# Store order, weight preparation and early splits around the attention bursts and the last quads of a fused attention and two-layer feed-forward kernel

## The chip, the cores and the metric

One core of a Trainium2 chip runs the whole program. TensorE (PE) multiplies, VectorE (DVE) and ScalarE (ACT) do the element-wise work, and one DMA queue, issued by SyncE (SP), moves everything between DRAM and on-chip memory. The metric is the device time of one execution in microseconds. Three runs of the kernel before gave a median of 1045.58 us (1045.37 to 1046.80).

## The reference

Attention over chunks of 32 queries with 16 keys to the left, 8 to the right and 8 memory keys, then two feed-forward layers over 3072 tokens:

```python
scores = scale * q_c @ k_full.T; a = exp(scores - max); a = a / (sum(a) + 1e-09)
x = (a @ v_full) as 3072 x 512
h = x @ w_in;  x = (s * max(h, 0)**2 + b) @ w_out          # 512 -> 2048 -> 512
h = x @ w_in2; out = (h - tanh(h)) @ w_out2                # 512 -> 2048 -> 512
```

## The kernel before, in words

Every float32 product is made of three TensorE products of rounded parts (`three`, lines 238 to 241): high weight by high input, low weight by high input, high weight by low input. So each operand is first split into a rounded high part on ACT and the remainder on DVE. The first two of the three need only the high part of the input, the third its low part. Large products use a seven-product scheme (P1 to P7) instead of eight; the combinations of weights and inputs that it needs are made on DVE.

Four stages follow one another. First attention runs in 24 units of 128 queries, side by side with **up 1** (x by w_in, ReLU, square). Then **down 1** multiplies the squares by w_out, **up 2** by w_in2 with tanh, and **down 2** by w_out2. Every engine works its own instructions in the order in which the program lists them; this order is written out by hand, there is no scheduler. A wait on one engine therefore holds all that stands behind it on that engine.

**START** (lines 38 to 54) is a list of tokens, one step each, for units 0 to 17 and the first 36 turns of up 1. `F` is the product of one turn (12 matmuls), `r` its ReLU on ACT, `Q` its square (on ACT for the turns of SCALAR_SQUARES, else on DVE), `k` and `K` the two halves of a combination on DVE, `st` the store of four squared turns. `wl`, `ws`, `wf`, `wd`, `wc` and `ww` prepare w_in2: load of a raw block, scaling on ACT, filling on DVE, a store, four sums on DVE in the raw block's place, and a store of these. `wr` is `w1_sums` (line 973): five DVE instructions that combine one block of w_in into tile Z8, and a store of it.

**The loop** at line 1066 makes the turns n = 36 to 79 of up 1. At the turns of BURSTS (44, 51, 58, 65, 70) `burst` (line 514) puts a block of attention in front of the turn: scores of two units on PE, their masks on DVE (line 395), the value products of two earlier units on PE, then the transposes of two units on PE. Transposes go into the PSUM banks of the new scores, so they wait until the masks have read these. P2_STEPS gives the turns at which the remaining w_in2 blocks are loaded, scaled, filled and summed; QUADRANTS the turns at which a block of w_out is loaded (with its place), begun on ACT and ended on DVE. EXTRAS holds single steps, among them `w1_sums` 6 and 7 at turns 38 and 41, and `ws_high`, `ws_low` of the first quad at turn 78.

**The quads** (line 1173) make the last part of up 1 by the seven-product scheme, s = 0 to 3. The squares of quad s are written into tiles `oa` and `ob`; there are two pairs of these tiles, so quad 3 writes where quad 1 wrote and must wait until the stores of quad 1 have landed. The stores of quad s - 1 are issued by `combos(1)` inside quad s, four DMAs of 384 and 512 KB. `copy(3)` writes into `oa` and reads a PSUM bank that the product P3 then adds to, so P3 waits for it. `load_to` loads parts of down 1 (1 MB each in two DMAs, `load1`, line 882) into four places, B_STREAM.

**Down 1** takes each part in two halves ("entries"). `split` rounds a half on ACT (line 762) and makes the remainder on DVE (line 763) into a ring of three places, B_RING; `multiply` is 12 matmuls per entry. Entries 0 and 1 use the first half of the weights, entries 2 and 3 the second, made by `high` on ACT and `low` on DVE. `run` (line 811) splits entries 0 to 2, multiplies entry 0, then calls `between1`, which finishes quad 3 with six DVE instructions, and then splits entry 3.

Of the kernel before, what the change touches and what calls it, by code (L numbers as in the profile page):

```python
# [8 lines left out]
F32 = mybir.dt.float32  # L9
# [36 lines left out]
st0 vv8 E11 M12 V7 S13 o7 T9 Q8 M13 r11 R13 F12 F13 E13 l7 qk15 X7 R10 Q11 qk14 K1 C9 wl1 F14 S15  # L46
vv11 D13 D11 L7 M15 R15 S14 Q9 Q10 ws1 r13 r12 M14 V9 E15 V8 T13 T11 st1 wf1 F15 C11 wc1 qk17 r14
D15 k2 Q12 V11 Q14 S17 r15 X11 L11 wl0 vv13 F18 M17 ww1 wd1 F17 R17 E10 Q13 D10 K2 Q15 X9 C13 X8 r17
T10 L9 T15 C10 R14 vv10 V13 L8 V10 k3 C15 r18 K3 F16 r16 R12 F21 wl2 X10 st2 E12 F19 Q16 L10 Q18 Q17
wr4 r19 r21 F20 F24 Q19 wr5 r20 E14 F22 r22 qk16 D12 st3 Q20 F23 r23 Q21 ws2 F25 k4 Q22 F26 ws0 Q23  # L50
wf2 K4 r24 r26 F27 wd2 st4 D14 k5 r25 K5 Q24 wc2 F28 Q25 Q26 r27 F29 ww2 st5 Q27 F30 r29 r28 Q29 k6
K6 r30 st6 Q28 F31 F32 X13 Q30 r31 L13 T12 T14 Q31 r32 k7 K7 Q32 F35 r35 F34 Q35 C12 r34 F33 vv12
Q34 wf0 r33 st7 wc0 S16 V12 Q33 k8 K8 wd0 ww0 st8 X12 M16 L12 R16 C14
"""

WEIGHTS2 = {
# [47 lines left out]
PLAIN_EXPONENTIALS = set()  # L104

P2_STEPS = {}
for m, at in ((3, (42, 45, 46, 50)), (4, (50, 53, 54, 57)), (5, (57, 60, 61, 64)), (6, (64, 67, 68, 71)),
              (7, (71, 74, 75, 78))):
    for step, n in zip(("load", "scaled", "filled", "sums"), at):
        P2_STEPS.setdefault(n, []).append((step, m))  # L110

# [1 line left out]
PLACE_IN_ORDER = list(range(UP_FIRST, 72)) + list(range(80, 88))  # L113
BURSTS = {44: 18, 51: 20, 58: 22, 65: 24, 70: 26}
QUADRANTS = {
    37: ("E8", 40, 41), 45: ("E9", 48, 49), 53: ("E8", 55, 56), 59: ("E9", 61, 62), 66: ("E8", 68, 69),
    73: ("E9", 76, 77), 78: ("E9", None, None),
}
QUADRANT_BEGINS = {x[1] for x in QUADRANTS.values()}
# [33 lines left out]
def tile_chunk_attention_two_ffn(  # L153
# [42 lines left out]
    def new(place, n, dt, name):  # L196
        assert n <= SIZE[place[0]], (place, n)
        if place[0] in "QSRYWV":
            assert place[0] in side["letters"], place
        pool = arena if place[0] in "EZ" else side["of"]  # L200
        return pool.tile([P, n], dt, tag=place, name=name)
# [41 lines left out]
    def scaled(z, raw):  # L243

        hi32 = raw.rearrange("p (n two) -> p n two", two=2)[:, :, 1]
        nc.scalar.activation(
            out=z, in_=hi32.bitcast(F32), func=AF.Prelu, bias=0.0, scale=2.0 ** -112, alpha=2.0 ** 32
        )
# [11 lines left out]
    def filled_in_raw(z, raw):  # L260
# [6 lines left out]

    A_W = [f"E{n}" if n != 3 else "E11" for n in range(8)]
    A_RAW = ("E8", "E9")
    P2_RAW = ("E9", "E8", "E8", "E8", "E9", "E8", "E9", "E8")  # L270
    A_QK, A_V = ("Q0", "Q1", "Q2"), ("Z0", "Z1", "Z2")
    A_X = (("E10", "E3"), ("E12", "E13"))
    A_FULL = ("Q0", "Q1")
# [6 lines left out]
          ("A22", 0): "Z11", ("A22", 1): "Z5", ("A12", 0): "Z0", ("A12", 1): "Z1"}  # L280
    B_S = (("Z2", "Z3"),)
    B_WHL = (("E8", "E10"), ("E0", "E1"))
    B_STREAM = ("E11", "E9", "E2", "E3")
    B_RING = ("E4", "E5", "E12")
    B_ACC = {"W": ("W0", "W0", "Y0"), "X": ("Y1", "Y2", "Y3"), "T3": ("Y4", "Z2", "Z3"), "Q": ("Y4", "Z11", "Z5")}
    X2 = {
# [3 lines left out]
    }  # L290
    C_WORDS, C_W, C_KEEP = "E3", ("Y1", "Y2", "Z5", "V0"), "E5"
    C_OA, C_OB = ("E12", "E10"), "W0"
# [250 lines left out]
    def load_raw(src, n, place):  # L543
        raw = new(place, 2048, I32, "raw")
        nc.sync.dma_start(out=raw, in_=src.bitcast(I32)[n])
        return raw
# [70 lines left out]
    def up1_combine(g, half):  # L617
        combine(*(t.rearrange("p s k t -> p s (k t)") for t in oab[g]), nc.vector, half)

    def up1_store(g):  # L620
        (oa, ob), (j, q) = oab.pop(g), (tile_at(4 * g)[0], tile_at(4 * g)[1] // 4)
        nc.sync.dma_start(out=o1[j][:, q, 0:3], in_=oa[:, 1:4].rearrange("p s k t -> p s (k t)"))
        nc.sync.dma_start(out=o1[j][:, q, 3:7], in_=ob.rearrange("p s k t -> p s (k t)"))
# [294 lines left out]
    def part1(step, g):  # L918
# [9 lines left out]
        else:  # L928
# [7 lines left out]
    down1 = DownInPlace(  # L936
        wo1, Z1, B_S, B_WHL, B_STREAM, B_RING, load1,
        lambda part, e: part.rearrange("p (b k t) -> p b k t", b=2, k=4)[:, :, 2 * e:2 * e + 2].rearrange(
            "p b k t -> p b (k t)"
        ),  # L940
        lambda t: lambda k: t[:, :, HB * k:HB * (k + 1)],
        b_c[:, 0:1], final1, (0, 1), 1, ORDER1, WEIGHTS1, [(g, h) for g in range(NG) for h in range(2)],
    )

    p2_raw, p2_z = {}, {}

    def p2_load(n):
        p2_raw[n] = load_raw(wi2, n, P2_RAW[n])

    def p2_scaled(n):  # L950
        p2_z[n] = new("Z5" if n in (1, 2) else "Z6", 1024, F32, "zw")
        scaled(p2_z[n], p2_raw[n])

    def p2_filled(n):
# [18 lines left out]
    def w1_sums(n):  # L973
# [18 lines left out]
        "r": up1_relu, "Q": up1_square,  # L992
        "k": lambda q: up1_combine(q, 0), "K": lambda q: up1_combine(q, 1), "st": up1_store,
        "wl": p2_load, "ws": p2_scaled, "wf": p2_filled, "wc": p2_sums, "wd": p2_store,
        "ww": p2_store_sums,
    }
# [19 lines left out]
    for u in (14, 15):  # L1016
        load_v(u)
    p2 = {"load": (p2_load,), "scaled": (p2_scaled,), "filled": (p2_filled, p2_store), "sums": (p2_sums, p2_store_sums)}
    quads = []
    t_hl, ws_hl, w1_words = {}, {}, {}  # L1020
# [28 lines left out]
    def ws_high(s):  # L1049
        w = ws_hl[s] = new(A_WS[s], 2048, F32R, "ws")  # L1050
        nc.scalar.activation(out=w[:, 0:1024], in_=w1_words[s], func=AF.Copy)

    def ws_low(s):
        w = ws_hl[s]
        hi, lo = w[:, 0:1024], w[:, 1024:2048]
        minus(lo, w1_words.pop(s), hi.bitcast(F32))
        ws_hl[s] = tuple(t.rearrange("p (q c m) -> p q c m", q=4, c=2) for t in (hi, lo))

    EXTRAS = {
        38: [(w1_sums, 6)], 41: [(w1_sums, 7)],  # L1060
        71: [(ws_load, 0), (ws_load, 1), (t_sum, "T3"), (t_sum, "T2")], 72: [(t_sum, "T1"), (t_split, "T1")],
        73: [(t_sum, "T4"), (ws_load, 2)], 74: [(t_split, "T3")], 76: [(t_split, "T2")],
        77: [(t_split, "T4"), (ws_load, 3)], 78: [(ws_high, 0), (ws_low, 0)],
# [108 lines left out]
    q.mult("P7")  # L1172
    for s, q in enumerate(upq):
        p, r = upq[s - 1] if s else None, upq[s + 1] if s + 1 < QUADS else None
        if s == 2:
            down1.load_to(2)
        q.mult("P6")
        if p:
            p.add(3)
            p.square(3)  # L1180
        if r:
            ws_high(s + 1)
        q.copy(2)
        if p:
            p.combos(0)
        else:
            up1_combine(21, 0)
        if s == 0:
            quads[0].begin()
            quads.append(down1.load_quadrant("E8"))  # L1190
        if s == 1:
            quads[1].begin()
        if s == 3:
            down1.high(0, 0)
        q.mult("P2")
        q.add(1)
        if s == 3:
            down1.load_to(3)
        if r:
            ws_low(s + 1)  # L1200
        else:
            down1.low(0, 0)
        q.mult("P5")
        q.copy(3)
        q.square(1)
        q.add(2)
        if p:
            p.combos(1)
        else:
            up1_combine(21, 1)  # L1210
            up1_store(21)
        if r:
            r.mult("P1")
            r.copy(1)
        else:
            down1.high(0, 1)
            down1.low(0, 1)
        q.mult("P3")
        q.square(0)
        if s in (1, 2):  # L1220
            quads.pop(0).end()
        if s == 2:
            down1.sums(0, 0)
            down1.sums(0, 1)
        if r:
            r.mult("P7")
        q.square(2)
        if s == 3:
            down1.split(0)
        q.mult("P4")  # L1230

    swap_side("WYV")
# [196 lines left out]
    for s in range(NQ - 1):  # L1429
        q, p, r = quads2[s], quads2[s - 1] if s else None, quads2[s + 1]  # L1430
        n, g = q.n, q.g
# [202 lines left out]
```

## Time and profile before

| | |
|---|---|
| median of three runs | 1045.58 us |
| the profiled execution, its own time | 1046.08 us |
| its span, first to last instruction | 1044.2 us |
| PE busy | 1017.2 us, 97% |
| DVE busy | 805.6 us, 77% |
| ACT busy | 604.7 us, 58% |
| moved by DMA | 273.12 MB, mean 262 GB/s |
| chain that ended last | PE 80%, DVE 8%, DMA 7%, ACT 4% |

PE is busy nearly all the time, so the chain that ended last runs mostly along PE. What an edit can win is PE's idle time and the stretches in which PE's granted clock is low; the idle time of DVE, ACT or the queue counts only where PE waits for them. 1.9 us of the execution's own time lie outside its span.

### The profile page before, as it was taken

The numbers are of one execution on the slowest core, as the hardware profiler recorded it, in microseconds if no ns is written. First come the engines' busy times: TensorE is split into PE (matmuls) and PEld (weight loads), VectorE is DVE, ScalarE is ACT, GpSimd is POOL, SyncE is SP. The second block draws the span as 40 slices with busy tenths as digits, with TensorE's granted clock in tenths as the row PEclk, the third lists the DMA queues.
The fourth block names the chain that finished last, engine by engine and source line by source line (L and its number), as shares of the span: only waits on it lengthen the run. The fifth ranks groups of instructions, "written<-read, shape, count | busy, mean of one in ns | idle before, by whom it ended". The sixth has DMA issues, their size and how long they took to land.

```text
span 1044.2 us, 15640 instructions
## 1 busy us (share of the span) xinstructions
PE 1017.2 (97%) x6088; PEld 840.2 (80%) x6088; DVE 805.6 (77%) x989; ACT 604.7 (58%) x1106; POOL 12.2 (1%) x53
## 2 busy tenths in 40 slices
PE   7999999999999799999999999999999999999998
PEld 5888778877878588888888888888888888888887
DVE  7998557887677779889788788888888976776654
ACT  8998645657677575666556554545545554444432
POOL 1000000000000000000000000000000000000000
PEclk9999999999999899999999999999999999999999
DMA  8899587897888897796654165556659996656771
GB/s 344 304 327 315 218 356 288 348 348 277 314 346 288 302 376 243 256 374 225 216 186 143 41 235 221 217 224 252 243 215 343 361 348 202 194 187 224 246 256 61
DMA packets 85930, 273.12 MB, mean 262 GB/s; under 512 B 5984, under 2 KB 13408, under 8 KB 75104
## 3 DMA queue, kind: packets, MB, share of 16 engines
q1 hardware_dynamic: 85856, 272.13, 71.2%
q8 instruction: 47, 0.77, 0.3%
q14 instruction: 27, 0.22, 0.1%
HBM read 163.06 MB, written 109.05 MB: 261 GB/s over the span
## 4 chain that ended last, share of the span: by engine, by line
PE 80%; DVE 8%; DMA 7%; ACT 4%; issue 1%; SPq 0%; ACTq 0%; DVEq 0%
PE pb L239 26%; PE pb L241 26%; PE pb L240 26%; DMA raw<-in_wo_dram 3%; DMA o<-oa 2%; ACT sm L413 1%; DVE ob L627 1%; DVE sm L395 1%; PE pb L372 1%; DVE oa L615 1%; PE pb L481 1%; DVE ws L893 1%; DMA v<-in_vw_dram 1%; PE pb L444 1%; DVE xl L503 1%
## 5 line engine op out<-in xcount | busy, mean ns | idle before, releaser
L239 PE MATMUL pb<-ringhringl,whl 128*128 128x512 f32 (+1 forms) x680 | 263.5, 387 | 1.9 <-ACT ringhringl L762 1.9
L241 PE MATMUL pb<-ringhringl,whl 128*128 128x512 f32 (+1 forms) x680 | 263.5, 387 | 0.4 <-DVE ringhringl L763 0.4
L240 PE MATMUL pb<-ringhringl,whl 128*128 128x512 f32 (+1 forms) x680 | 263.4, 387 | 0.0
L767 ACT ACTIVATE ringhringl<-part 128x1024 fp32r<-128x1024 f32 x120 | 127.0, 1060 | 148.9 <-PE pb L241 145.8
L768 DVE TENSOR_TENSOR ringhringl<-part,ringhringl 128x1024 fp32r<-128x1024 f32 x120 | 146.8, 1223 | 73.3 <-ACT ringhringl L767 73.0
L239 PEld LDWEIGHTS pb<-ringhringl,whl 128*128 128x128 f32 x680 | 128.0, 188 | 28.3 <-ACT ringhringl L762 2.3
L241 PEld LDWEIGHTS pb<-ringhringl,whl 128*128 128x128 f32 x680 | 128.0, 188 | 27.2 <-DVE ringhringl L763 1.0
L240 PEld LDWEIGHTS pb<-ringhringl,whl 128*128 128x128 f32 x680 | 128.0, 188 | 25.9
L239 PE MATMUL pb<-xh,w 128*128 128x512 f32 (+1 forms) x344 | 135.4, 394 | 3.3 <-ACT r L601 2.5
L240 PE MATMUL pb<-xh,w 128*128 128x512 f32 (+1 forms) x344 | 132.8, 386 | 0.1
L241 PE MATMUL pb<-xl,w 128*128 128x512 f32 (+1 forms) x344 | 132.6, 385 | 0.0
L239 PE MATMUL pb<-x2hx2l,w 128*128 128x512 f32 x224 | 87.1, 389 | 0.0
L241 PE MATMUL pb<-x2hx2l,w 128*128 128x512 f32 x224 | 87.1, 389 | 0.0
L240 PE MATMUL pb<-x2hx2l,w 128*128 128x512 f32 x224 | 87.1, 389 | 0.0
L239 PEld LDWEIGHTS pb<-xh,w 128*128 128x128 f32 x344 | 64.8, 188 | 19.8 <-ACT r L601 3.3
L762 ACT ACTIVATE ringhringl<-part,b_c 128x1024 fp32r<-128x1024 f32 x48 | 54.9, 1151 | 37.1 <-PE pb L241 35.3
L241 PEld LDWEIGHTS pb<-xl,w 128*128 128x128 f32 x344 | 64.9, 189 | 13.3
L240 PEld LDWEIGHTS pb<-xh,w 128*128 128x128 f32 x344 | 64.9, 189 | 12.5 <-DVE w L571 0.3
L1386 ACT ACTIVATE pb<-oa 128x512 f32<-128x512 f32 x72 | 43.1, 599 | 53.7 <-DVE oa L1378 52.7
L601 ACT ACTIVATE r<-pb 128x512 f32<-128x512 f32 x80 | 46.7, 593 | 43.9 <-PE pb L241 43.2
L413 ACT ACTIVATE sm<-sm,nmx 128x96 f32<-128x96 f32 x192 | 69.1, 366 | 4.7 <-DVE nmx L405 3.9
L763 DVE SCALAR_TENSOR_TENSOR ringhringl<-part,b_c,ringhringl 128x1024 fp32r<-128x1024 f32 x48 | 61.2, 1281 | 13.1 <-ACT ringhringl L762 13.0
(182 smaller groups left out, 1497.9 us busy)
## 6 DMA issues: line engine op xcount, KB each, us to landing
part<-o SPq DMA_DIRECT2D x84, 512.0 KB, 5.2
part<-o SPq DMA_DIRECT2D x42, 1024.0 KB, 6.0
o<-oa SPq DMA_DIRECT2D x24, 1024.0 KB, 3.9
o<-ob SPq DMA_DIRECT2D x20, 1024.0 KB, 7.1
o<-ob SPq DMA_DIRECT2D x24, 768.0 KB, 5.3
raw<-in_wi_dram SPq DMA_DIRECT2D x16, 1024.0 KB, 7.4
raw<-in_wo_dram SPq DMA_DIRECT2D x16, 1024.0 KB, 8.6
o<-oa SPq DMA_DIRECT2D x20, 768.0 KB, 6.1
```

The lines of the kernel that those rows point to most:

```text
L239: nc.tensor.matmul(acc, lhsT=whi, rhs=xhi, start=first, stop=False, skip_group_check=more)
L240: nc.tensor.matmul(acc, lhsT=wlo, rhs=xhi, start=False, stop=False, skip_group_check=more)
L241: nc.tensor.matmul(acc, lhsT=whi, rhs=xlo, start=False, stop=last, skip_group_check=more)
L372: nc.tensor.matmul(score_bank(u, g)[QE * e:QE * (e + 1), KE * (r0 + r):KE * (r0 + r + 1)], lhsT=tq[sl, r, QE * e:QE * (e + 1)], rhs=tk[sl, ...
L395: nc.vector.scalar_tensor_tensor(out=of_half(sm_t[u], w, True), in0=of_half(scores_of(u), w, True), scalar=scale, in1=m8, op0=ALU.mult, op ...
L413: nc.scalar.activation(out=sm[:, h, :], in_=sm[:, h, :], func=AF.Exp, bias=nmx[:, h:h + 1], scale=1.0, **({"accum_out": sums[:, h:h + 1]} ...
L601: nc.scalar.activation(out=r, in_=up_ps[p], func=AF.Relu)
L762: nc.scalar.activation(out=xh, in_=src, func=AF.Identity, bias=self.bias)
L763: nc.vector.scalar_tensor_tensor(out=xl, in0=src, scalar=self.bias, in1=xh.bitcast(F32), op0=ALU.add, op1=ALU.subtract)
L767: nc.scalar.activation(out=xh, in_=src, func=AF.Copy)
L768: nc.vector.tensor_tensor(out=xl, in0=src, in1=xh.bitcast(F32), op=ALU.subtract)
L1386: nc.scalar.activation(out=self.rs[o], in_=src, func=AF.Tanh)
```

## The change

Four things are moved; the arithmetic stays.

1. Quads: the parts of down 1 are loaded behind the stores of the quad before instead of ahead of them. Part 0 is now loaded already in quad 1, parts 1 and 2 in quad 2, part 3 in quad 3. For this, parts 0 and 2 swap their places in B_STREAM, and the places of U in X2 with them.
2. Loop: the steps of w_in2 and w_out get the same distance to every burst. The sums of w_in2 now stand three turns ahead of the next burst instead of one or none. All raw blocks of w_in2 from the second on go into place E8, all blocks of w_out in the loop into E9. Block 2 of w_in2 moves from START into turns 38, 39 and 41, its load to a later place in START.
3. `w1_sums` 6 and 7 move from turns 38 and 41 into START.
4. Quad 3: entries 0 and 1 of down 1 are split ahead of the second half of the weights, entry 0 ahead of P3 and entry 1 behind it.

```diff
-T10 ... R12 F21 wl2 X10 st2 ... F23 r23 Q21 ws2 F25 k4 Q22 F26 ws0 Q23
-wf2 K4 r24 r26 F27 wd2 st4 D14 k5 r25 K5 Q24 wc2 F28 Q25 Q26 r27 F29 ww2 st5 Q27 F30 r29 r28 Q29 k6
-K6 r30 st6 Q28 F31 F32 X13 Q30 r31 L13 T12 T14 Q31
+T10 ... R12 F21 X10 st2 ... F23 r23 Q21 F25 wr6 k4 Q22 F26 ws0 Q23
+K4 r24 r26 F27 st4 D14 k5 r25 K5 Q24 F28 Q25 Q26 r27 F29 wr7 st5 Q27 F30 r29 r28 Q29 k6
+K6 r30 st6 Q28 F31 F32 X13 Q30 r31 wl2 L13 T12 T14 Q31
...
-for m, at in ((3, (42, 45, 46, 50)), (4, (50, 53, 54, 57)), (5, (57, 60, 61, 64)), (6, (64, 67, 68, 71)),
-              (7, (71, 74, 75, 78))):
+for m, at in ((2, (None, 38, 39, 41)), (3, (42, 45, 46, 48)), (4, (49, 52, 53, 55)), (5, (56, 59, 60, 62)),
+              (6, (63, 66, 67, 69)), (7, (70, 72, 73, 75))):
...
-    37: ("E8", 40, 41), 45: ("E9", 48, 49), 53: ("E8", 55, 56), 59: ("E9", 61, 62), 66: ("E8", 68, 69),
+    38: ("E9", 41, 42), 45: ("E9", 48, 49), 52: ("E9", 55, 56), 59: ("E9", 62, 63), 66: ("E9", 69, 70),
...
-    P2_RAW = ("E9", "E8", "E8", "E8", "E9", "E8", "E9", "E8")
+    P2_RAW = ("E9",) + 7 * ("E8",)
...
-    B_STREAM = ("E11", "E9", "E2", "E3")
+    B_STREAM = ("E2", "E9", "E11", "E3")
...
-        p2_z[n] = new("Z5" if n in (1, 2) else "Z6", 1024, F32, "zw")
+        p2_z[n] = new("Z5" if n == 1 else "Z6", 1024, F32, "zw")
...
-        38: [(w1_sums, 6)], 41: [(w1_sums, 7)],
...
-        if s == 2:
-            down1.load_to(2)
         q.mult("P6")
...
-        if s == 3:
-            down1.load_to(3)
...
             p.combos(1)
+            down1.load_to(s if s > 1 else 0)
...
         else:
-            down1.high(0, 1)
-            down1.low(0, 1)
+            down1.split(0)
         q.mult("P3")
+        if s == 3:
+            down1.split(1)
         q.square(0)
...
         if s == 3:
-            down1.split(0)
+            down1.high(0, 1)
+            down1.low(0, 1)
         q.mult("P4")
```

## Rows read from the trace of the kernel before

**Rows 1.** Windows: PE, PEld, DVE, ACT, POOL busy (x), PE clock, DMA share, GB/s.

```profile
238.00:240.00 2.00, 2.00 (x16) 1.57 (x13) 2.00 (x4) 1.78 (x6) 0.00 (x0) 0.50 0.99 303
...
340.00:360.00 20.00, 12.97 (x42) 9.40 (x41) 12.32 (x16) 10.20 (x13) 0.00 (x0) 0.83 0.89 315
...
360.00:1040.00 680.00, 680.00 (x3020) 563.78 (x3020) 530.78 (x590) 352.15 (x428) 0.00 (x0) 1.00 0.65 235
```

**Rows 2.** Waits of PE from 90 to 365 us: total, times, longest.

```profile
PE pb L239 <- ACT oa L1142: 4.8, 1, 4.8
PE pb L444 <- DVE sm L395: 3.8, 6, 1.8
PE pb L239 <- ACT r L601: 2.5, 2, 1.4
PE pb L239 <- ACT ringhringl L762: 1.9, 1, 1.9
PE pb L239 <- DVE oa L615: 0.9, 2, 0.6
PE pb L240 <- DVE ws L893: 0.7, 1, 0.7
```

**Rows 3.** Timeline of PE, quad 3 into down 1: start, duration, line [idle before].

```profile
341.30 0.39 PE L241 MATMUL pb<-tl,ws 128*128 128x512 f32 x1
346.44 0.79 PE L239 MATMUL pb<-xh,ws 128*128 128x512 f32 x1 [4.76 <-ACT oa L1142]
...
352.94 0.54 PE L239 MATMUL pb<-ringhringl,whl 128*128 128x512 f32 x1 [1.91 <-ACT ringhringl L762]
...
357.08 0.39 PE L239 MATMUL pb<-ringhringl,whl 128*128 128x512 f32 x1
```

**Rows 4.** Chain that ended last, 335 to 346 us: start, duration, what.

```profile
335.15 10.54 DMA o<-oa
345.80 0.61 ACT oa L1142
```

**Rows 5.** Timeline of the DMA issues on SP in quad 2.

```profile
328.07 4.74 SPq L884 DMA_DIRECT2D part<-o  x6
```

**Rows 6.** DMA issues, 280 to 365 us: size of each, median us to landing.

```profile
part<-o SPq DMA_DIRECT2D x10, 512.0 KB, 6.9
...
o<-oa SPq DMA_DIRECT2D x8, 384.0 KB, 4.8
```

**Rows 7.** Timeline of ACT, the first splits of down 1.

```profile
351.76 3.21 ACT L762 ACTIVATE ringhringl<-part,b_c 128x1024 fp32r<-128x1024 f32 x3
```

**Rows 8.** Timeline of DVE, the first splits of down 1.

```profile
352.92 3.68 DVE L763 SCALAR_TENSOR_TENSOR ringhringl<-part,b_c,ringhringl 128x1024 fp32r<-128x1024 f32 x3 [2.23 <-ACT ringhringl L762]
...
360.38 1.28 DVE L763 SCALAR_TENSOR_TENSOR ringhringl<-part,b_c,ringhringl 128x1024 fp32r<-128x1024 f32 x1
```

**Rows 9.** Timeline of PE, the end of the burst at turn 58.

```profile
236.62 0.65 PE L444 MATMUL pb<-ident,sm 64*96 64x64 f32 x16 [1.77 <-DVE sm L395]
...
238.50 0.79 PE L239 MATMUL pb<-xh,w 128*128 128x512 f32 x1
...
240.96 0.40 PE L239 MATMUL pb<-xh,w 128*128 128x512 f32 x1
```

**Rows 10.** Timeline of DVE ahead of the bursts at turns 44 and 51.

```profile
179.90 1.21 DVE L977 TENSOR_TENSOR ws<-w 128x1024 f32<-128x1024 f32 x1
...
182.86 1.28 DVE L615 TENSOR_TENSOR oa<-pb,r 128x512 f32<-128x512 f32 x2
...
207.33 0.42 DVE L965 TENSOR_TENSOR raw<-zw 128x256 f32<-128x256 f32 x1
...
...
209.39 1.81 DVE L395 SCALAR_TENSOR_TENSOR sm<-pb,mask_mid 128x768 f32<-128x768 f32 x2
```

**Rows 11.** Timeline of ACT in START, the scaling of block 2 of w_in2.

```profile
124.97 1.11 ACT L246 ACTIVATE zw<-raw 128x1024 f32<-128x1024 f32 x1
```

**Rows 12.** Longest waits of the DMA issues on SP, 280 to 365 us.

```profile
SPq L545 <- DMA w2z<-raw: 7.4, 1, 7.4
```

More of the change, by code (lines that the diff above doesn't have):

```diff
@@ L48 @@
 D15 k2 Q12 V11 Q14 S17 r15 X11 L11 wl0 vv13 F18 M17 ww1 wd1 F17 R17 E10 Q13 D10 K2 Q15 X9 C13 X8 r17
-T10 L9 T15 C10 R14 vv10 V13 L8 V10 k3 C15 r18 K3 F16 r16 R12 F21 wl2 X10 st2 E12 F19 Q16 L10 Q18 Q17
-wr4 r19 r21 F20 F24 Q19 wr5 r20 E14 F22 r22 qk16 D12 st3 Q20 F23 r23 Q21 ws2 F25 k4 Q22 F26 ws0 Q23
-wf2 K4 r24 r26 F27 wd2 st4 D14 k5 r25 K5 Q24 wc2 F28 Q25 Q26 r27 F29 ww2 st5 Q27 F30 r29 r28 Q29 k6
-K6 r30 st6 Q28 F31 F32 X13 Q30 r31 L13 T12 T14 Q31 r32 k7 K7 Q32 F35 r35 F34 Q35 C12 r34 F33 vv12
-Q34 wf0 r33 st7 wc0 S16 V12 Q33 k8 K8 wd0 ww0 st8 X12 M16 L12 R16 C14
+T10 L9 T15 C10 R14 vv10 V13 L8 V10 k3 C15 r18 K3 F16 r16 R12 F21 X10 st2 E12 F19 Q16 L10 Q18 Q17 wr4
+r19 r21 F20 F24 Q19 wr5 r20 E14 F22 r22 qk16 D12 st3 Q20 F23 r23 Q21 F25 wr6 k4 Q22 F26 ws0 Q23 K4
+r24 r26 F27 st4 D14 k5 r25 K5 Q24 F28 Q25 Q26 r27 F29 wr7 st5 Q27 F30 r29 r28 Q29 k6 K6 r30 st6 Q28
+F31 F32 X13 Q30 r31 wl2 L13 T12 T14 Q31 r32 k7 K7 Q32 F35 r35 F34 Q35 C12 r34 F33 vv12 Q34 wf0 r33
+st7 wc0 S16 V12 Q33 k8 K8 wd0 ww0 st8 X12 M16 L12 R16 C14
 """
```

2 rows, old and new, of the table X2 are left out of this document.

## The prediction

> **What bounds the kernel now.** I read the page first (PE busy 97% of the span), then the windows, to see where the missing 3% lie. From 360 us on PE has no idle time and the full clock [rows 1], so nothing can be won there, and every microsecond won before 360 us is kept as long as transfers and DVE follow. In 340 to 360 us PE is busy for 12.97 of 20 us and its granted clock averages 0.83 [rows 1]; this is the quads' end and down 1's start. The waits of PE between 90 and 365 us name the causes [rows 2]: one of 4.8 us for `copy(3)`, six of 3.8 us together in which transposes wait for masks, two of 2.5 us for a ReLU, 1.9 us for the first split, 0.9 us for squares on DVE, 0.7 us for the low part of the first quad's weights. Each belongs to one part of the change. 680 us with 3020 matmuls [rows 1] make 0.225 us for one; single steps in the timeline are 0.227, which I use.
>
> **Quads, what is lost.** Between the matmul at 341.30 and that at 357.08, the tenth of entry 0, lie 22 steps [rows 3]: 6 of P3, 6 of P4, 10 of down 1. At 0.227 they take 5.0 us; they took 15.8. So 10.8 us are lost: the two long waits (4.76 and 1.91 [rows 3]), smaller ones, and the slow clock behind both.
>
> **Quads, the stores.** `copy(3)` of quad 3 waits for quad 1's `oa` store, issued at 335.15, which took 10.54 us [rows 4], against a median of 4.8 for its kind [rows 6]. What stood ahead of it on the one queue are six loads of 512 KB, 328.07 to 332.81 [rows 5]. The change leaves two of the six there and puts four behind. The store's issue time does not move, since SP waits there for quad 2's combination on DVE. With 4.8 us it lands at about 340.0. P5's last matmul starts at 341.30 and takes 0.39 [rows 3], so `copy(3)` can start at 341.7, 1.7 us after the landing. It takes 0.61 and PE follows at once [rows 4]: P3 starts at 342.4 instead of 346.44. The 0.8 us that stay are not a transfer: nothing stands between P5 and P3 in quad 3.
>
> **Quads, the splits.** P3 and P4 are 12 matmuls, so entry 0 can begin at 345.1. Split 0 stands on ACT behind `copy(3)` and two squares of like size, some 1.9 us by the 0.61 of the copy, then takes 1.16 (351.76 to 352.92, when DVE starts [rows 7, 8]): 344.8. Its low part on DVE ends 1.3 us later, at 346.1, and the third matmul of entry 0 needs it, a gap of some 0.5 us. Entries 0 to 2 then run to 354.0. What is late next is **split 3**. The second half of the weights now stands on ACT behind two splits (three took 3.21 [rows 7]) and four squares. From `copy(3)` to the splits ACT took 5.96 us before [rows 4, 7], of which 0.5 was waiting; with two splits of 1.03 added, `high(0, 1)` ends at about 341.7 + 5.4 + 2.1 = 349.2. DVE then has `low(0, 1)` and split 2, 1.2 each (three splits took 3.68), the six instructions that finish quad 3, 3.8 (356.6 to 360.38), and split 3, 1.28 [rows 8]: 349.2 + 2.4 + 3.8 + 1.3 = 356.8. PE wants it at 354.5, the third matmul of entry 3. So 2.3 us of a new wait; entry 3 ends at 356.8 + 0.1 + 10 x 0.227 = 359.2. Before, it ended 39 steps behind 357.08, at 365.9. Gain 6.7 at full clock.
>
> The clock may fall again. Behind a wait of 1.77 us the granted clock was 0.50, that is 1.2 GHz, and the six steps from 238.50 to 240.96 took 2.46 instead of 1.36 [rows 1, 9]: 1.1 us. Behind 352.94 nine steps took 4.14 instead of 2.04 [rows 3], of which some 0.5 is waiting: 1.6. A wait of 2.3 us is longer than the first of these, so I take the fall: gain 6.7 - 1.4 = **5.3**. Bounds: 6.7 with full clock, 9 if split 3 is not late at all, 2.5 if the store again takes 10.54 us (then P3 stays at 346.4 and only the splits' order is won).
>
> The Trainium skill, "DMA: Bandwidth & Descriptors", section "Rules for kernel authors", says to issue a DMA early, compute, and wait on its semaphore late. It speaks against the part of this change that puts loads of down 1 later. The rows agree that a load has a long way (6.9 us [rows 6]), yet they show that here the early loads cost the store behind them more. What the rule would make of the time is rival 2.
>
> **Bursts.** Masks come late because DVE is still at weight work. Ahead of turn 44 it is `w1_sums` 7, from 179.90 to 182.86; ahead of turn 51 it is the four sums of w_in2, from 207.33, and one square of 0.6, with the masks only at 209.39 [rows 10], so the sums took 1.46; turn 58 is built like 51 and waits 1.77 [rows 9]. The change takes `w1_sums` (3.0 us) out of turns 38 and 41 and moves the four sums (1.46 us) to turns 48 and 55, ahead of the wait for the w_out block, where DVE has idle time. Block 2 of w_in2 comes in at turns 38 to 41 instead, at most 3.9 us on DVE (the sums' 1.46 and two full-width instructions of 1.21 at most), against 6.0 removed. So the masks of turn 44, which had to wait until 184.1 (182.86 and 1.28), come 2 us earlier. At turn 51 the masks move forward by 1.46 and all waiting for them goes; at turn 58 the wait falls from 1.77 to about 0.3, since the w_out block still lands late. Of 3.8 us [rows 2] 0.5 stays. Behind the shorter wait at turn 58 I expect no fall of the clock: that gives back 1.1. Around each removed gap PE restarts with some 0.1 less. Gain 3.3 + 1.1 + 0.4 = **4.8**; from 2.5 (one burst alone mends) to 5.5.
>
> **START.** The scaling of block 2 (1.11 us on ACT [rows 11]) stood ahead of the ReLU for which PE waits; the second of the two waits (2.5 less 1.4, so 1.1 us [rows 2]) goes with it. The first stays: it hangs on a store that the edits don't touch. The wait for a square on DVE (0.6 [rows 2]) stood behind the four sums and a store behind block 2's store; both are gone. What may take its place is `w1_sums` 7, whose 3 us on DVE and store now precede `st5` on SP, and two turns later a square waits for that store. Gain **1.6**, from 0.7 (that wait returns) to 2.0. `w1_sums` 6 runs while ACT still waits for that store, when DVE has nothing else to do, and costs nothing; without that cover it would cost its 3.0 us.
>
> **Turn 78.** The last sums of w_in2 move from 78 to 75; they stood right ahead of `ws_low`. Gain **0.7** [rows 2], with nothing below 0.5.
>
> **The sum.** 5.3 + 4.8 + 1.6 + 0.7 = 12.4 us. The profiled execution took 1046.1 us; that gives 1033.7. The median of the runs lies 0.5 lower: **1033.2**.
>
> **Rivals.**
> 1. *Split 3 is not late, or the clock stays up.* DVE's chain has 2 us of idle time while it waits for `high(0, 1)`; if ACT is there earlier, the wait goes. Quads 6.7 to 9: 1029.5 to 1032. Against it: DVE's order is fixed, and its instructions alone fill the stretch.
> 2. *The loads become the wait.* Parts 1 and 2 are now issued behind quad 1's last store, at about 336 to 339 with 0.8 us for each of four (4.74 for six [rows 5]), and split 2 wants part 1 at 349. With 6.9 us [rows 6] they land at 346; with 10.54 [rows 4] at 349.5, nearly late; or the store itself stays slow, since two loads still precede it. Quads 2.5 and the rest: 1036. With half of the bursts' gain missing as well: 1038.5.
> 3. *Nothing is won.* Loads of down 1 and later stores follow bytes, not PE: in 340 to 360 us the DMA engines are busy 0.89 of the time [rows 1]. If down 1 then waits for parts, the early start is given back: 1045.5. Against it: from 360 us on their share is 0.65, and PE never waited there [rows 1].
> 4. *Slower.* All raw blocks of w_in2 now share E8, so the load of block m stands on SP until the stored sums of block m - 1 have landed. That wait was 7.4 us once [rows 12], and behind it on SP stand the next burst's q, k and v and the store of a finished group; a late store holds squares, as in START, where such a wait cost PE up to 3.4 us (2.5 and 0.9 [rows 2]). Five loads at 3.4 are 17: 1046.1 - 12.4 + 17 = 1050.7. It decides only if a hold exceeds the two groups of turns, some 20 us, until a tile comes back. For sums three turns ahead of the burst I expect holds of 4 to 5 us.
>
> **How the numbers follow.** Forecast 0.55, rival 1 0.15, rival 2 0.18, rival 3 0.06, rival 4 0.06. The range takes the forecast's bounds, rival 1 and rival 2: 1029 to 1039. Some 0.2%, 2.1 us, is what a measurement of this kernel can tell from no change. Faster by more 0.88, within it 0.06, slower 0.06.
>
> **What would show it.** Right: quad 1's last `oa` store lands in about 5 us and `copy(3)` no longer waits for it; P3 starts some 1 us behind P5; the longest remaining wait of PE in down 1's start is for split 3's low part on DVE, and the clock dips behind it; transposes of turns 44 and 51 don't wait; the ReLU wait in START is single. Wrong: PE waiting for a part, for q, k or v, or anywhere behind 365 us, or a square in turns 48 to 60 waiting for a store.

## The result and the profile after

The changed kernel takes 1033.86 us in the median of four runs (1033.32 to 1035.07), against 1046.19 of the kernel before (four runs, 1045.37 to 1047.71): a ratio of 0.9882, 95% interval 0.9865 to 0.9899. That is 12.3 us less. The forecast took 12.4 off the profiled execution of before and 0.5 more for the median: 1033.2.

The profiled execution of after is the longest of its four: 1035.07 us, with a span of 1033.3. Against the profiled 1046.08 of before that is only 11.0 us; the ledger below shows where the rest went.

Waits of PE from 90 to 365 us in after (total, times, longest), to be held against [rows 2]:

```profile
PE pb L241 <- DVE ringhringl L763: 2.0, 1, 2.0
PE pb L239 <- ACT r L601: 0.7, 1, 0.7
PE pb L239 <- DVE oa L615: 0.7, 2, 0.5
PE pb L239 <- ACT oa L1141: 0.7, 1, 0.7
PE pb L481 <- DMA v<-in_vw_dram: 0.7, 1, 0.7
PE pb L444 <- DVE sm L395: 0.5, 2, 0.3
PE pb L481 <- DVE oa L615: 0.4, 1, 0.4
PE pb L240 <- DVE ws L893: 0.2, 1, 0.2
PE pb L239 <- DVE xl L503: 0.2, 1, 0.2
```

`copy(3)` falls from 4.8 to 0.7, the transposes from 3.8 in six to 0.5 in two, the ReLU from 2.5 in two to 0.7 in one. The first split is gone; a new 2.0 stands at the top, the low part of a split. The wait for v was 0.2 in before (it stands below the lines that [rows 2] show). Windows of after, in the columns of [rows 1]:

```profile
340.00:350.00 10.00, 8.80 (x37) 6.61 (x36) 8.00 (x11) 7.56 (x9) 0.00 (x0) 1.00 1.06 391
350.00:360.00 10.00, 9.14 (x33) 7.38 (x34) 8.36 (x8) 4.23 (x4) 0.00 (x0) 0.83 1.05 388
360.00:1030.00 670.00, 670.00 (x2979) 555.41 (x2977) 521.51 (x582) 345.25 (x422) 0.00 (x0) 1.00 0.64 234
```

From 360 us on PE has no gap, as in before, so what is won ahead of it is kept. One stretch, 350 to 360, still has a lowered clock.

**The ledger.** The 4200 products of width 512 and 256 stand in the same order in both traces. The difference between the starts of the same product is the time won up to there. A step in this difference belongs to what stands at it:

| from the start of the span to | after minus before, us | step |
|---|---|---|
| 97 us, identical code | +1.44 | +1.44 |
| 101 us, a wait for v | +1.96 | +0.52 |
| START done (product at 140.74 before, 140.63 after) | -0.11 | -2.07 |
| bursts 44, 51, 58 done (at 234.95 after) | -5.78 | -5.67 |
| turn 71, behind the last burst (275.08 after) | -5.45 | +0.33 |
| turn 78 (301.74) | -5.71 | -0.26 |
| in entry 0 of down 1 (341.46) | -15.10 | -9.39 |
| down 1 at full clock (356.72) | -11.04 | +4.06 |
| last product | -10.89 | +0.15 |

The first line is no effect of the change: the code is the same up to there, and the profiled runs of e1 to e6 and of e8 below, which share it, stand within 0.6 us of before at that point. The second line is probably the change's own. Timelines of SP in before, then in after:

```profile
97.66 0.33 SPq L545 DMA_DIRECT2D raw<-in_wi_dram  x1
98.05 0.43 SPq L622 DMA_DIRECT2D o<-oa  x1
```

```profile
96.03 1.19 SPq L622 DMA_DIRECT2D o<-oa  x1
```

In before SP stood at `wl2` until 97.66, and the store of `st2` went out behind it at 98.05. The change takes `wl2` away from there, so this store goes out at 96.03, 1.1 us behind the load of v (issued at 94.94) for which PE waits at 102.00. In the seven kernels with after's START that load took 5.95 to 7.60 us to land and PE waited up to 1.28 for it; in before, e1 and e2 it took 6.12 to 6.44 and PE waited 0.17 at most. No run tests this alone.

From there on START is worth 2.1 (1.55 if the wait for v is charged to it), the bursts 5.67 - 0.33 = 5.3, turn 78 0.3, the quads 9.39 - 4.06 = 5.3: 13.0 in all, or 12.5 with the wait for v. Without the late opening of 1.44 the profiled execution would have taken 1033.6; the median is 1033.86.

The timeline of PE in after, quad 3 into down 1, the places of [rows 3]:

```profile
335.58 0.39 PE L241 MATMUL pb<-tl,ws 128*128 128x512 f32 x1
336.65 0.50 PE L239 MATMUL pb<-xh,ws 128*128 128x512 f32 x1 [0.69 <-ACT oa L1141]
...
339.53 0.39 PE L239 MATMUL pb<-ringhringl,whl 128*128 128x512 f32 x1
...
350.86 0.50 PE L241 MATMUL pb<-ringhringl,whl 128*128 128x512 f32 x1 [2.02 <-DVE ringhringl L763]
...
352.33 0.63 PE L240 MATMUL pb<-ringhringl,whl 128*128 128x512 f32 x1
...
354.46 0.63 PE L239 MATMUL pb<-ringhringl,whl 128*128 128x512 f32 x1
```

P3 starts 1.07 us behind P5's last product, where it was 5.14; entry 0 follows with no long gap; split 3's low part costs 2.02, and behind it the five products from 352.33 to 354.46 take 0.43 us each, not 0.227. The timelines of SP, ACT and DVE in after say why:

```profile
329.43 0.46 SPq L1163 DMA_DIRECT2D o<-oa  x1
329.94 2.40 SPq L1164 DMA_DIRECT2D o<-ob  x1
332.39 2.65 SPq L884 DMA_DIRECT2D part<-o  x4
```

```profile
336.00 0.60 ACT L1141 ACTIVATE oa<-pb 128x512 f32<-128x512 f32 x1 [1.08 <-PE pb L241]
...
342.10 1.14 ACT L857 ACTIVATE whl<-zq,sign 128x1024 fp32r<-128x1024 f32 x1
```

```profile
343.27 1.29 DVE L860 SCALAR_TENSOR_TENSOR whl<-zq,sign,whl 128x1024 fp32r<-128x1024 f32 x1 [1.93 <-ACT whl L857]
344.47 1.28 DVE L763 SCALAR_TENSOR_TENSOR ringhringl<-part,b_c,ringhringl 128x1024 fp32r<-128x1024 f32 x1
...
348.93 0.69 DVE L627 TENSOR_TENSOR ob<-ob,oa 128x512 f32<-128x512 f32 x1
349.53 1.28 DVE L763 SCALAR_TENSOR_TENSOR ringhringl<-part,b_c,ringhringl 128x1024 fp32r<-128x1024 f32 x1
```

The store of `oa` (329.43) now stands ahead of four loads, not behind six, and `copy(3)` (336.00) waits for PE's bank alone. DVE stands idle 1.93 us for the high part of the second half of the weights, then works without a gap: its low part, split 2, the six instructions that finish quad 3, and split 3 at 349.53. It is the chain that the prediction wrote down, to within half a microsecond at each place.

### The profile page after: what moved, and what is told of

Same layout as the page of the kernel before. It is cut to its first block, busy times and chain, and to the rows that moved or that the text cites. A ratio compares the mean times of both kernels' runs of the same rounds, so it can differ in the third digit from the quotient of the medians.

```text
span 1033.3 us, 15642 instructions
## 1 busy us (share of the span) xinstructions
PE 1015.0 (98%) x6088; PEld 838.5 (81%) x6088; DVE 806.0 (78%) x989; ACT 602.5 (58%) x1106; POOL 12.7 (1%) x53
## 4 chain that ended last, share of the span: by engine, by line
PE 81%; DVE 8%; ACT 5%; DMA 4%; issue 2%; SPq 0%; DVEq 0%; ACTq 0%
PE pb L239 26%; PE pb L241 26%; PE pb L240 26%; DVE ob L627 1%; ACT sm L413 1%; DVE sm L395 1%; DMA raw<-in_wo_dram 1%; DMA raw<-in_wi_dram 1%; ACT r L601 1%; PE pb L481 1%; DMA v<-in_vw_dram 1%; DMA o<-oa 1%; PE pb L372 1%; DMA qk<-in_qk_dram 1%; ACT pt L452 1%
## 5 line engine op out<-in xcount | busy, mean ns | idle before, releaser
L240 PEld LDWEIGHTS pb<-xh,w 128*128 128x128 f32 x344 | 64.7, 188 | 12.5 <-DVE w L571 0.3
```

The source lines that it names most:

```text
L240: nc.tensor.matmul(acc, lhsT=wlo, rhs=xhi, start=False, stop=False, skip_group_check=more)
```

## The experiments

Theory: four separate causes, each with the price of the forecast; in the quads the place of the loads ahead of the store, then DVE's fixed order. Rivals: in the quads it is the traffic itself and not the place; the two edits of the quads cover the same idle time; the bursts' gain comes from `w1_sums` and not from the sums' place. All kernels do the whole work. Those of e1 to e4 ran beside the kernel before on one chip (before: median 1045.93), those of e5 to e8 on another (1045.61). Beside after, before took 1046.19, so a comparison of after with e1 to e8 carries some 0.3 to 0.6 us of this difference. Where a gain is given for one stretch of a trace, it is read as in the ledger.

**e1: before, with the loads behind the stores alone.**

```diff
-    B_STREAM = ("E11", "E9", "E2", "E3")
+    B_STREAM = ("E2", "E9", "E11", "E3")
...
-        if s == 2:
-            down1.load_to(2)
...
-        if s == 3:
-            down1.load_to(3)
...
             p.combos(1)
+            down1.load_to(s if s > 1 else 0)
```

> The kernel before with only the loads of down 1 put behind the stores (part 1 of the change). Theory: the order on the one queue is what made quad 1's store late. Its last oa store lands within about 5 us instead of 10.5, copy(3) of quad 3 waits for P5 alone, P3 starts about 0.8 us behind P5's end instead of 4.9. The first split stays behind the second half of the weights, so PE waits some 3 us for it with a fall of the clock behind; entry 3 of down 1 ends some 4 us earlier against the rest. Time 1041.5 to 1042.5. Rival (the store is slow because of the sheer traffic, not of its place): the wait for copy(3) stays above 3 us and the time within 1 us of before.

1041.03 us (1039.08 to 1042.51), ratio 0.9953 (0.9934 to 0.9973). Timeline of PE in e1:

```profile
342.22 0.50 PE L239 MATMUL pb<-xh,ws 128*128 128x512 f32 x1 [0.69 <-ACT oa L1142]
347.81 0.80 PE L239 MATMUL pb<-ringhringl,whl 128*128 128x512 f32 x1 [2.52 <-ACT ringhringl L762]
```

The store takes 5.98 us from issue to landing (335.00 to 340.98) instead of 10.54, and `copy(3)` no longer waits for it. So the place of the loads was the cause and not the traffic as such: the bytes are the same. The first split, still behind the weights on ACT, then waits 2.52 instead of 1.91, with the slow clock behind it; the quads gain 3.7, where some 4 were expected. The time lies 0.5 us below the range that was expected.

**e2: before, with the splits first alone.**

```diff
-            down1.high(0, 1)
-            down1.low(0, 1)
+            down1.split(0)
         q.mult("P3")
+        if s == 3:
+            down1.split(1)
...
         if s == 3:
-            down1.split(0)
+            down1.high(0, 1)
+            down1.low(0, 1)
```

> The kernel before with only the splits of entries 0 and 1 ahead of the second half of the weights (part 4 of the change). Theory: the wait of 4.8 us for copy(3) stays; the wait of 1.9 us for the first split goes; a wait of about 1.3 us for split 3's low part on DVE appears in entry 3, since the six instructions that end quad 3 stand ahead of it. Gain 2 to 3 us: 1043 to 1044. Together with the loads alone this makes 6 to 7 us, more than the 5.3 us that both gave in the changed kernel, because split 3's wait is paid by the one that makes PE earlier. Rival (the two parts are independent and add up): 1044.7 or more, no new wait in entry 3.

1043.11 us (1041.76 to 1046.93), ratio 0.9985 (0.9969 to 1.0000): at this interval no clear difference, so the quads are read from its trace.

```profile
345.35 0.80 PE L239 MATMUL pb<-xh,ws 128*128 128x512 f32 x1 [5.09 <-ACT oa L1142]
360.46 0.50 PE L241 MATMUL pb<-ringhringl,whl 128*128 128x512 f32 x1 [1.34 <-DVE ringhringl L763]
```

The store's wait stays, the first split's is gone, split 3's is new at 1.34 as expected, with no slow clock behind it. From P5's last product on the quads gain 1.65, less than the 2 to 3 expected. With e1's 3.7 that makes 5.4, and both edits together gave 5.3 in after: they add up. I had expected the sum of the single gains to lie clearly above the joint one; it doesn't, because e2 alone gained less than I thought.

**e3: after, with the quads of before.**

```diff
-    B_STREAM = ("E2", "E9", "E11", "E3")
+    B_STREAM = ("E11", "E9", "E2", "E3")
...
+        if s == 2:
+            down1.load_to(2)
...
-            down1.load_to(s if s > 1 else 0)
...
-            down1.split(0)
+            down1.high(0, 1)
+            down1.low(0, 1)
...
```

> The changed kernel with the quads of before: only START, the turns of w_in2 and w_out and the moved weight sums (parts 2 and 3 of the change). Theory: START gives about 1.5 us, the bursts about 5.3 (transposes of turns 44 and 51 don't wait for masks, no fall of the clock at turn 58), turn 78 0.3 to 0.7; the quads lose 10.8 us as before. Time 1038.5 to 1039.5. Rival (what the bursts win is taken back by the quads, since their transfers follow bytes): 1043 or more, with a longer wait for copy(3) than 4.8 us.

1038.92 us (1036.72 to 1040.24), ratio 0.9924 (0.9895 to 0.9953). The `copy(3)` wait is back at 4.2. The rest of the change, without the quads, is so worth about 7 us, and after's remaining 5 are the quads'. In this run the burst at turn 58 hardly gained: 0.44 us against 2.4 in after. Timelines of ACT and PE there:

```profile
226.16 1.17 ACT L246 ACTIVATE zq<-raw 128x1024 f32<-128x1024 f32 x1 [4.81 <-DMA raw<-in_wo_dram]
```

```profile
226.09 1.55 PE L372 MATMUL pb<-qk 64*64 64x96 f32 x64
229.97 1.15 PE L481 MATMUL pb<-pt,v 96*64 96x64 f32 x32 [1.25 <-DVE oa L615]
231.43 1.95 PE L444 MATMUL pb<-ident,sm 64*96 64x64 f32 x32 [0.31 <-DVE sm L395]
```

The w_out block lands, and its scaling starts, just as the burst begins (226.16, 226.09); filling and a square on DVE are then late for the value products. The granted clock was 0.50 from 231.4 to 234.7, so the expected "no fall of the clock at turn 58" did not come here.

**e4: after, with split 3 ahead of quad 3's last instructions on DVE.** The last six instructions of quad 3 go behind split 3 (four) and split 4 (two), P7's weight sums two entries later, and the loads of parts 4 and 5 with the stores.

```diff
-    (0, 1): [("sums", 2, 0)], (0, 2): [("sums", 2, 1)], ...
+    (0, 3): [("sums", 2, 0)], (0, 4): [("sums", 2, 1)], ...
...
-        if p == 0 and k == 0:
+        if p == 0 and k == 1:
             upq[-1].add(3)
             upq[-1].square(3)
             upq[-1].combos(0)
+        if p == 0 and k == 2:
             upq[-1].combos(1)
...
+    down1.skip = (1,)
     down1.run(between1)
```

> The changed kernel with quad 3's last six DVE instructions moved behind split 3 (four of them) and split 4 (two), the weight sums of P7 two entries later, and the loads of parts 4 and 5 put off by two entries, as they need quad 3's stores. Theory: the wait of 2.0 us for split 3's low part and the fall of the clock behind it vanish; PE runs from entry 1 on with no wait over 0.3 us: 3.5 us less than the changed kernel, 1030 to 1031. Rival (split 3 is late because of its data, part 1 of down 1, or of ACT): a wait of about 2 us stays in entry 3 or moves into entry 4, and the time stays within 1 us of the changed kernel. If the later loads are late, PE waits for a part in entries 8 to 11.

1031.92 us (1031.25 to 1032.56), ratio 0.9864 (0.9842 to 0.9886). The 2.02 wait and the slow clock behind it are gone: 3.9 us, where 3.5 were expected. But 1.84 are given back at entry 8, by waits alone: the granted clock stays at 1.00. Timelines of PE, ACT and SP in e4:

```profile
361.07 0.50 PE L239 MATMUL pb<-ringhringl,whl 128*128 128x512 f32 x1 [0.82 <-ACT ringhringl L762]
362.39 0.50 PE L241 MATMUL pb<-ringhringl,whl 128*128 128x512 f32 x1 [0.59 <-DVE ringhringl L763]
```

```profile
359.87 1.15 ACT L762 ACTIVATE ringhringl<-part,b_c 128x1024 fp32r<-128x1024 f32 x1 [5.84 <-DMA part<-o]
```

```profile
352.30 4.82 SPq L884 DMA_DIRECT2D part<-o  x6
```

Six loads go out only at 352.30, behind the late stores, and part 4 lands 6.3 us after its issue, too late for its split. So putting loads behind stores wins only while the load is early enough.

**e5: e4, with part 4 loaded ahead of those stores.**

```diff
+        if p == 0 and k == 0:
+            down1.load_to(4)
         if p == 0 and k == 1:
```

> The kernel of e4_split3 with part 4 loaded two entries earlier again (it doesn't need quad 3's stores), only part 5 behind them. Theory: the waits of 0.8 and 0.6 us at entry 8 in e4_split3 came from part 4, issued only behind quad 3's stores; they go, and with them a fall of the clock, and the whole gain of split 3 stays: from entry 1 of down 1 to entry 12 PE has no wait over 0.3 us; about 1.8 us less than e4_split3, 1030 us. Rival (the queue is full and any load there is late): waits of 0.5 us or more stay at entries 8 to 11, and quad 3's stores land later.

1032.28 us (1030.43 to 1032.97), ratio 0.9872 (0.9856 to 0.9889). In the trace both waits of entry 8 are gone: e5 loses 0.36 over the products over which e4 lost 1.84. Some 0.7 is lost again at entry 12, behind a wait of 0.49 for a split's low part (372.49), where none over 0.3 was expected. The median did not fall with it: the expected 1030 was reached by the profiled run alone (1030.43). What e5 adds to e4 is so seen in the trace only and not in the times. Its turn 58 waited 0.95 us for the value products; e4's 0.5.

**e6: after, with the sums of blocks 3 and 4 back at turns 50 and 57.**

```diff
-for m, at in ((2, (None, 38, 39, 41)), (3, (42, 45, 46, 48)), (4, (49, 52, 53, 55)), (5, (56, 59, 60, 62)),
+for m, at in ((2, (None, 38, 39, 41)), (3, (42, 45, 46, 50)), (4, (50, 52, 53, 57)), (5, (57, 59, 60, 62)),
```

> The changed kernel with only the four sums of blocks 3 and 4 of w_in2 back at turns 50 and 57, right ahead of the bursts (the loads of blocks 4 and 5, which need their place, at 50 and 57). Theory: it was the place of the sums on DVE that made the masks late: at turn 51 the transposes wait 1.0 to 1.3 us again, at turn 58 the waits grow from 0.9 to 2 us or more with a fall of the clock behind; 2.5 to 4 us slower than the changed kernel, 1036.5 to 1038. Rival (the bursts got better because of other moves, loads and places): no new wait over 0.3 us at turn 51 and the time within 1 us of the changed kernel.

1039.13 us (1038.09 to 1039.76), ratio 0.9941 (0.9923 to 0.9958): 5.3 above after, more than the 2.5 to 4 expected, and with one place wrong. Nearly all of it comes at turn 58 (4.4 us from after's trace to e6's, with the granted clock at 0.50 from 232.0 to 238.7); turn 51 lost only 0.5. Timelines of PE (with the burst's first scores) and ACT at turn 58:

```profile
226.97 1.55 PE L372 MATMUL pb<-qk 64*64 64x96 f32 x64
231.30 1.48 PE L481 MATMUL pb<-pt,v 96*64 96x64 f32 x32 [1.70 <-DVE oa L615]
234.22 1.95 PE L444 MATMUL pb<-ident,sm 64*96 64x64 f32 x32 [1.45 <-DVE sm L395]
```

```profile
227.48 1.17 ACT L246 ACTIVATE zq<-raw 128x1024 f32<-128x1024 f32 x1 [5.25 <-DMA raw<-in_wo_dram]
```

1.45 is what the four sums take, as worked out in the prediction. The 1.70 is the late block; whether the edit had a part in its lateness, since the loads of two w_in2 blocks moved with the sums, isn't shown. At turn 51 the block landed 6.7 us ahead of the burst's first transposes (scaling at 199.53, transposes at 206.22); in before it was 5.6 (203.71 to 209.34, where PE began to wait). With that extra microsecond DVE had the sums behind it in time.

Both bursts follow one sum. Take the time that a burst puts between two products (the distance of their starts less the 0.227 of a step) and the lead of the w_out block (from the start of its scaling to the burst's first scores). They add up to 8.22 or 8.23 us where the sums stand right ahead of the burst (turn 51 in before, e1, e2 and e6, turn 58 in e1 and e2), and to 6.77 to 6.79 where they have been moved (turn 58 in after, e4, e5 and e7). Between them lie 1.45, the four sums. Where the clock fell inside turn 58 the sum is 0.45 to 0.5 more (before, e3, e6). Turn 51 is never shorter than 4.62, which after reaches with a lead of 2.87; with the sums ahead it would have taken 8.22 - 2.87 = 5.35. So the sums' place costs its 1.45 in full only where the block is late as well.

At turn 58 the wait of the value products for the square follows in the same way from how late the scaling of the block starts, counted from the burst's first scores. Six traces give the same difference, and in e8 the block is early and nothing waits for it:

| | scaling starts | scores start | difference | wait (L481) | wait less difference |
|---|---|---|---|---|---|
| e7 | 231.76 | 232.74 | -0.98 | 0.16 | 1.14 |
| after | 226.98 | 227.76 | -0.78 | 0.36 | 1.14 |
| e4 | 225.24 | 225.86 | -0.62 | 0.51 | 1.13 |
| e5 | 225.30 | 225.51 | -0.21 | 0.95 | 1.16 |
| e3 | 226.16 | 226.09 | +0.07 | 1.25 | 1.18 |
| e6 | 227.48 | 226.97 | +0.51 | 1.70 | 1.19 |
| e8 | 220.34 | 225.18 | -4.84 | none | |

**e7: after, with `w1_sums` 6 and 7 back at turns 38 and 41.** Block 2 of w_in2 stays at 38 to 41, so both stand there.

```diff
-... Q21 F25 wr6 k4 ... r27 F29 wr7 st5 Q27
+... Q21 F25 k4 ... r27 F29 st5 Q27
...
+        38: [(w1_sums, 6)], 41: [(w1_sums, 7)],
```

> The changed kernel with only the weight sums 6 and 7 back at turns 38 and 41, where block 2 of w_in2 now also stands. Theory: DVE gets 6 us more ahead of turn 44, and the masks there come 2 to 4 us late: PE waits that long at turn 44; in START the wait of 0.5 us for a square goes. 2 to 4 us slower than the changed kernel, 1036 to 1038. Rival (DVE has room for both): waits at turn 44 stay under 0.5 us, the time falls by the 0.5 us of START.

1037.15 us (1036.24 to 1041.32), ratio 0.9930 (0.9905 to 0.9954): 3.3 above after: the size expected, but not the wait expected. Timeline of PE at turns 43 and 44, and the window there:

```profile
179.26 0.50 PE L239 MATMUL pb<-xh,w 128*128 128x512 f32 x1 [1.80 <-DVE oa L615]
...
188.22 0.65 PE L444 MATMUL pb<-ident,sm 64*96 64x64 f32 x16 [0.31 <-DVE sm L395]
```

```profile
178.00:184.00 6.00, 4.74 (x24) 3.41 (x28) 5.83 (x13) 0.47 (x2) 0.00 (x0) 0.72 0.80 327
```

DVE is busy 5.83 of 6 us: too full, a square 1.80 us late at turn 43, the clock at 0.72 in the mean, then small waits for masks (0.31 and 0.21, where 2 to 4 us were expected). Since block 2 of w_in2 stands there as well, this is not turn 44 of before: it shows that DVE has no room for both, not what each costs. By the end of turn 44 e7 stands 5.0 us behind after; 1.6 of it come back in down 1, where its clock stays up (last section). The 0.47 wait of after in START is gone with `wr7`; but e4 and e5, with after's START, don't show it either, so that alone doesn't name its cause.

**e8: the findings joined.** e5, with `st5` ahead of `wr7`, a second tile for the odd `w1_sums`, and the w_out block of turn 52 loaded at 51.

```diff
-... r27 F29 wr7 st5 Q27
+... r27 F29 st5 wr7 Q27
...
-    38: ("E9", 41, 42), 45: ("E9", 48, 49), 52: ("E9", 55, 56),
+    38: ("E9", 41, 42), 45: ("E9", 48, 49), 51: ("E9", 55, 56),
...
-        t = new("Z8", 1024, F32, "ws")
+        t = new("Z8" if n % 2 == 0 else "Z7", 1024, F32, "ws")
```

> e5_part4 with three more edits at waits that the changed kernel keeps: in START the store of group 5 ahead of weight sum 7; weight sums 5 and 7 in tile Z7, so that sum 5 doesn't wait for sum 4's store; the block of w_out for turns 55 and 56 loaded at turn 51 instead of 52, ahead of turn 52's stores. Theory: the square's wait of 0.5 us goes (its store is issued earlier), the ReLU's wait of 0.7 us shrinks to 0 to 0.4, the 0.9 us at turn 58 go since the block lands earlier: 1.5 to 2 us less than e5_part4, 1028 to 1029. Rival (a DVE in order and not the block sets turn 58): its waits stay; (the first store hangs on traffic): the ReLU's wait stays; then 1030.

1028.43 us (1027.82 to 1029.70), ratio 0.9840 (0.9825 to 0.9855): 17.2 us under the kernel before beside it and 5.4 under after's median, below every run of both. Waits of PE in e8 from 90 to 400 us:

```profile
PE pb L481 <- DMA v<-in_vw_dram: 1.1, 1, 1.1
PE pb L239 <- ACT oa L1141: 0.7, 1, 0.7
PE pb L241 <- DVE ringhringl L763: 0.3, 1, 0.3
```

Behind these come four more of 0.3 us or less. The ReLU waits of START are gone, as is the square's, and turn 58 keeps one of 0.17. The longest wait left, 1.07 for v at 101.11, is of the kind that the ledger ascribes to the moved `wl2`: the store of `st2` goes out at 94.56, 1.1 us behind that load. The three edits ran together, so what each gives is read from the trace alone.

## Why the prediction was right, point by point

**The total** came to 0.7 us of the forecast, and none of the rivals happened. Of the terms the quads' is right step by step. The others are off by 0.5 (bursts), 0.5 (START) and -0.4 (turn 78), and the half microsecond that PE lost in waiting for v had no term at all; that these cancel in part is luck. One sign that the prediction named for being wrong did come: PE waits for v, 0.68 us at 102.00 where it was 0.17. It did so ahead of the loop, not behind the holds of rival 4 from which the sign was drawn.

**Quads, 5.3 forecast, 5.3 measured.** Each step stands, to within half a microsecond. The store no longer holds `copy(3)`: the gap ahead of P3 fell by 4.1, as forecast (346.44 to 342.4, shown by e1 alone). What stays between P5 and P3 is 0.69 of waiting; I gave 0.8. The new wait for split 3 is 2.02; I gave 2.3 (my sum of 349.2, 2.4, 3.8 and 1.3 is 356.7, not 356.8). The slow clock behind it cost 1.8 (the ledger from -12.82 at 350.86 to -11.04 at 356.72); I gave 1.4. e4 takes that wait away and gains 3.9, the sum of both and 0.1. Rival 2, with its 2.5 for the quads, did not come: among the waits of after there is none for a part.

**Rival 2's mechanism is real elsewhere.** The Trainium skill, "DMA: Bandwidth & Descriptors", section "Rules for kernel authors", says to issue a DMA early and wait late. e1 shows the exception: early loads ahead of a store that frees a buffer cost 4.1 us. e4 shows the rule: loads behind late stores cost 1.8 at entry 8, and e5's earlier part 4 takes 1.5 of that away. Both are one queue and one order; what decides is which of them is wanted first.

**Bursts, 4.8 forecast, 5.3 measured, the mechanism only partly mine.** Turn 44 gained 1.47. The 3.3 of the prediction held only the 0.5 that its masks waited; with them went a wait of 0.46 for the value products (183.60 in before), which [rows 2] leave out. e7 shows that DVE has no room there for `w1_sums` beside block 2. Turn 51 gained 1.54, by the sum found in e6 0.7 of it through the sums' place and 0.8 because the w_out block had a lead of 2.87 and not of 2.07, which I had not forecast. Turn 58 gained 1.48 and 0.94 from the clock, as forecast. But the step "the sums ahead of the wait for the w_out block" is only half of it: the wait depends on when that block lands, and in e3 the same code gained 0.44. That the forecast came true there is luck: after's block landed 9.8 us after its issue (217.18 to 226.98), not 10.7 as in e3 (215.50 to 226.16). The sums' move takes 1.45 away, not the dependence; e8 does, by loading the block one turn earlier. Behind the last burst, at turn 71, PE waits 0.2 for `xl` in all seven kernels with the new loop and in none with the old; the ledger's 0.33 stands there, and its cause wasn't tested.

**START, 1.6 forecast, 2.1 measured.** The two waits forecast to go were 1.1 and 0.6, so 1.7 rather than 1.6. The second ReLU wait went (1.04), the square's went (0.79). What I named as a possible replacement came in after, e3 and e6 (0.47 at 140.63 in after): a square waiting for `st5`, which now stands behind `wr7`. The first ReLU wait I had left at its size, since no edit touches the store on which it hangs; it fell from 1.40 to 0.74, which more than made up for the replacement. The runs do not bear that step out. With after's START the wait was 0.67 to 0.82 in six traces, with before's 1.40, 1.27 (e1) and 0.54 (e2). The store stands on SP behind the second store of `w1_sums`, whose sums wait until the first store of `w1_sums` has landed, since both use the one tile Z8. That first store took 3.0 us to land in all seven kernels with after's START, and 3.75, 3.5 and 2.6 in before, e1 and e2. What had been issued ahead of it, `wl2` and `st2`, had all landed by 111.5, 111.4 and 109.1 there (106.2 in after, where `wl2` is gone from this place). So the moved `wl2` may have its part in this as well; no run tests it alone. e8 gives the odd `w1_sums` a second tile, SP issues that store of squares at 115.96, against 116.83 in before, although its opening ran 1.1 us later, and the wait is gone.

**Turn 78, 0.7 forecast, 0.3 measured.** This term was mis-sized, and its stated floor of 0.5 was wrong: the wait fell from 0.69 to 0.25. In e2, with the loop of before, it was 1.79, so its size scatters too. I took the whole wait to hang on the sums right ahead of `ws_low`. Timelines of ACT and DVE in after:

```profile
297.26 1.07 ACT L1041 ACTIVATE th<-t 128x1024 fp32r<-128x1024 f32 x1 [1.08 <-DVE thtl L893]
...
299.38 1.05 ACT L1051 ACTIVATE ws<-words 128x1024 fp32r<-128x1024 f32 x1
```

```profile
300.46 1.23 DVE L893 TENSOR_TENSOR ws<-words,ws 128x1024 fp32r<-128x1024 f32 x1 [0.23 <-ACT ws L1051]
```

DVE is free 0.23 us before the high part is there: the next thing that is late is `ws_high` on ACT, behind the split `th`, which itself waited 1.08 for DVE. I had named no successor of that wait, and it took what was left.

**Rival 4, the hold of SP by the single place E8,** did not decide. In after, the loads waited for the stored sums like this (longest waits of SP, 140 to 320 us):

```profile
SPq L545 <- DMA w2z<-raw: 17.5, 5, 6.0
```

3.5 us on average, somewhat under the 4 to 5 forecast, and PE waited for nothing that stood behind them on SP: its only wait for v is at 102.00, ahead of all of them, and no square in turns 48 to 60 waited for a store.

## What to carry to other kernels

On a single queue, sort transfers by when their effect is wanted, a store by the time at which its buffer must be free; then look for the reader that stands next in each engine's order, since the waits that take over are to be found there (split 3 here, `ws_high` at turn 78). When a wait hangs on a transfer whose landing scatters by a microsecond, moving the work that follows it wins a fixed price (1.45 at turn 58); only moving the issue takes the dependence away (e8). And a load taken off a queue lets all that stands behind it go earlier: look what that will run beside (here the load of v).

## What the runs showed of the hardware

- **The clock behind a wait is not decided by the wait's length alone.** Behind 2.02 us of waiting for split 3 the granted clock of after was 0.50, that is 1.2 GHz. Behind the same wait of 2.04 us at the same place in e7 it stayed at 1.00, 2.4 GHz. The window of after, then PE's wait and the window of e7:

```profile
352.00:355.00 3.00, 3.00 (x9) 2.35 (x8) 3.00 (x3) 0.30 (x1) 0.00 (x0) 0.50 1.07 381
```


```profile
355.58 0.50 PE L241 MATMUL pb<-ringhringl,whl 128*128 128x512 f32 x1 [2.04 <-DVE ringhringl L763]
```

```profile
350.00:360.00 10.00, 7.96 (x34) 6.06 (x34) 9.93 (x12) 4.17 (x5) 0.00 (x0) 1.00 1.06 399
```

  It also stayed up behind 1.34 in e2, and fell behind 1.25 and 0.31 at turn 58 of e3, behind 1.77 there in before [rows 9] and behind 2.52 in e1. A fall cost 0.9 us (turn 58) to 1.8 us (down 1); a forecast has to carry it as a chance.
- **The same load lands at different times.** The w_out block of 1 MB ahead of turn 58 took, from its issue on SP to the start of its scaling, 9.5 us in before (220.47 to 229.93), 9.6 in e7, 9.8 in after, 10.0 in e4, 10.4 in e5, 10.7 in e3 and 11.2 in e6 (216.29 to 227.48), with ACT waiting for it each time. after, e3, e4 and e5 have the same code up to there, so 0.9 us of this is scatter alone. By the table of e6 each microsecond of this is one of waiting.
- **The first 97 us of one code** differed by up to 1.5 us between profiled runs: against before, e1 to e6 and e8 came 0.1 to 0.5 us later, after 1.4 and e7 1.5. Without the ledger from product to product this would have hidden 12% of the gain.
